# Folding w_phi with 32x32 operands at 16 positions of the TensorE array, in one group per slice

## The chip, the cores and the metric

The program runs on one core of one Trainium2 chip. The metric is device time in microseconds (us): the median of three runs. A profile is one further execution, recorded instruction by instruction; its span is the time from the first to the last instruction.

TensorE multiplies matrices (its rows in the profile are PE, and PEld for loading the stationary operand), VectorE is DVE, ScalarE is ACT, GpSimd is POOL, and SyncE (SP) issues nearly all transfers. The five engines run their own instruction queues in order and wait for each other through semaphores. TensorE writes to PSUM, which has eight banks of 512 f32 columns by 128 partitions.

## The reference

One pre-LayerNorm block: linear attention with a learned feature map, then an MLP with ReLU, both with a residual. B=1, S=2048, D=1024, 32 heads of 32, Dff=3584.

```python
qkv = (x @ wqkv).reshape(B, S, 3, H, Dh)              # x is layernorm(A_x)
pq = einsum("bhsd,hdf->bhsf", q, w_phi)                # w_phi: 32 x 32 per head
pk = einsum("bhsd,hdf->bhsf", k, w_phi)
phi_q = concat([softmax(pq), softmax(-pq)], -1)        # phi_k from pk likewise
kv = einsum("bhsf,bhsd->bhfd", phi_k, v)
z  = einsum("bhsf->bhf", phi_k)
o  = einsum("bhqf,bhfd->bhqd", phi_q, kv) / (einsum("bhqf,bhf->bhq", phi_q, z)[..., None] + 1e-6)
h  = x + o.reshape(B, S, D) @ wo
out = h + relu(layernorm(h) @ w1) @ w2
```

## The kernel before

**Folding.** q and k are used only through w_phi, so the kernel multiplies w_phi into the projection weights: for each head, 1024 x 32 columns of wqkv by a 32 x 32 matrix. This is done on the chip in eight slices p of 256 columns, 0 to 3 for the keys and 4 to 7 for the queries. The weights come transposed (wqkT: one row per output column); a slice is two tiles `wt` of 128 x 1024 (wt_load, L269), a tile holding four heads on its partitions. `bd` (L1125) holds eight block-diagonal 128 x 128 matrices with four heads' w_phi each. fold_mm (L276) makes one block k (128 of the 1024 rows of the weight) of a slice: two f32 matmuls with the 128 x 128 block of wt stationary and bd moving, so the result lies with the weight's rows on the partitions. fold_step (L281) does that into a `tp` bank, and ScalarE copies it to a tile `wp0` (L288, L291 with reordered columns for the queries). fold_store (L296) writes two blocks of 256 KB to a DRAM scratch (wpk or wpq), and fold_ready (L302) marks them as loadable.

**What uses it.** The program is a list of items; an item has eight steps k, and a step is three projection matmuls (mm3, L181 to L183: high x high, high x low, low x high, in a split-f32 format of 512 columns). The first 32 items project the keys and values of the first eight x tiles: slice s by items 8s to 8s+7 (kv_item), then 16 items for the queries, and again for the other eight x tiles. So step 8n+k stands for item n, step k. Weight blocks ("keys" in the class Units) are loaded to six `raw` buffers, split by ScalarE (high part, L124) and by VectorE or GpSimd (low part, L128) into a ring of ten places; a place is freed by the last use in the slice before. At most two places are free ahead of a change of slice, and the other six blocks are split as the old slice's last item lets go of its places.

**What stands beside.** Each kv item ends with kv_first (L409: ScalarE copies the values, VectorE takes maximum, minimum and differences from the bank), then kv_exp, kv_second and kv_z 11, 13 and 18 steps after the item's start, and kv_third (L442: small matmuls) for two or three items together. For the first eight x tiles LayerNorm runs one or two items ahead: ln_stats on VectorE, ln_power on GpSimd, ln_norm on ScalarE (L237), ln_turn on TensorE (L244, into `tp` banks), whose result ScalarE and VectorE split to xT (L177, L178). The table X_STEPS gives the steps of x tiles 1 to 6. GpSimd also makes sums of w1 and w2 blocks (t_sum, L350) between a 512 KB load and a 512 KB store through SP, one every ten steps from step 24, sums 7 to 10 steps after the load.

**What sets the order.** All is placed by hand: do(n, k, f) and when(step, f) attach a function to a step, and it is issued behind that step's three matmuls; within a step functions follow in the order of their registration, before the splits. Every engine runs its instructions in the order in which the program issued them. Fold steps of slices 1 to 7 (L928 to L939) stand at k = 6 of each item from 1 on, and at k = 2 too in items 3 to 5 and from 8 on: 56 in all, the last in item 30. Slice 0 is folded ahead of the first item (first_fold, L371).

PSUM: `mm` has four banks (projection results in turn), `tp` two, `ac` two.

Of the kernel before, what the change touches and what calls it, by code (L numbers as in the profile page):

```python
# [9 lines left out]
F32 = mybir.dt.float32  # L10
F32R = mybir.dt.float32r
AF = mybir.ActivationFunctionType
# [3 lines left out]
P = 128  # L16
# [7 lines left out]
NK = D // P  # L24
# [21 lines left out]
UP = (1, 5, 6, 2, 7, 3, 4)  # L46
DOWN = (1, 5, 6, 3, 7, 2, 4)
OPENS = (1, 5, 2)
BANK_OF = {6: 1, 7: 1, 4: 1, 3: 5}


# [88 lines left out]
def kernel(  # L140
# [12 lines left out]
    v, act, pool, pe, sp = nc.vector, nc.scalar, nc.gpsimd, nc.tensor, nc.sync  # L153
# [26 lines left out]
    def mm3(ps, a_hi, a_lo, b_hi, b_lo, first, last, more=False):  # L180
        pe.matmul(ps, a_hi, b_hi, start=first, stop=False, skip_group_check=more)  # L181
        pe.matmul(ps, a_hi, b_lo, start=False, stop=False, skip_group_check=more)  # L182
        pe.matmul(ps, a_lo, b_hi, start=False, stop=last, skip_group_check=more)  # L183
# [78 lines left out]
    fp = folds.enter_context(tc.tile_pool(name="fold", bufs=2))  # L262
# [3 lines left out]
    wt_of = {}  # L266
# [6 lines left out]
            eng.dma_start(t, wqkT[j])  # L273
            wt_of[p, i] = t

    def fold_mm(p, k, ps):  # L276
        for i in range(2):
            pe.matmul(ps[:, i * P:(i + 1) * P], wt_of[p, i][:, k * P:(k + 1) * P],  # L278
                      bd[:, (2 * p + i) % 8, :], start=True, stop=True)

    def fold_step(p, k):  # L281
        ps = tp_bank()[:, 0:256]
        fold_mm(p, k, ps)
        if k % 2 == 0:
            wp_of[p, k // 2] = fp.tile([P, 512], F32, name="wp0", bufs=3)
        sb = wp_of[p, k // 2][:, k % 2 * 256:(k % 2 + 1) * 256]
        if p < 4:
            act.activation(sb, ps, AF.Copy)  # L288
        else:

            act.activation(sb.rearrange("p (r c f) -> p c r f", r=2, c=4),  # L291
                           ps.rearrange("p (c r f) -> p c r f", r=2, c=4), AF.Copy)

    wp_of = {}

    def fold_store(p, j):  # L296

        r = (p - 4) % 2
        dst = wpk[p][2 * j:2 * j + 2] if p < 4 else wpq[(p - 4) // 2][2 * j:2 * j + 2, :, r * 256:(r + 1) * 256]
        sp.dma_start(dst.rearrange("k p f -> p k f"), wp_of.pop((p, j)).rearrange("p (k f) -> p k f", k=2))  # L300

    def fold_ready(p, j):  # L302

        for k in (2 * j, 2 * j + 1):
            if p < 4 or p % 2:
                folded.add(("kv", p, k) if p < 4 else ("q", (p - 4) // 2, k))

# [61 lines left out]
    first_ps = {}  # L369

    def first_fold(k):  # L371
        if k % 2 == 0:
            first_ps[k // 2] = (ac_bank, mm_bank)[k // 4]()
        fold_mm(0, k, first_ps[k // 2][:, k % 2 * 256:(k % 2 + 1) * 256])

    def first_keys(k):

# [12 lines left out]
        place[0] = k % 2 == 1  # L390

    def first_copy(j):
        wp_of[0, j] = fp.tile([P, 512], F32, name="wp0", bufs=3)
        act.activation(wp_of[0, j], first_ps.pop(j), AF.Copy)

    def ready(key):
        kind, s, k = key[0], key[-2], key[-1]
# [423 lines left out]

    d = {}
# [7 lines left out]
    def d_add(b, m, name, q):  # L830
        v.tensor_add(d[name, q], dbank[b, BANK_OF.get(m, m)][q], d[name, q])

# [23 lines left out]
    for b, tiles in enumerate(groups):  # L856
        for hf in range(2):

            pairs = b == 0 and hf == 0
            for j in range(0, 4, 2 if pairs else 1):  # L860
# [3 lines left out]
                for half in range(2):  # L864
                    n = item(wo_pair, tiles[j:j + 2], hf, half, keys=[("wo", hf, 4 * half + k // 2) for k in range(8)])
# [36 lines left out]
    for t in range(1, NT):  # L902
        n = t - 1 if t < HT else q_n[1, t - HT] + 1
# [19 lines left out]

    for i, j in enumerate((2, 3, 0, 1)):
        do(1 + i // 2, 2 + 4 * (i % 2), first_copy, j)
        when(8 * (1 + i // 2) + 2 + 4 * (i % 2) + 3, fold_store, 0, j)
        when(40, fold_ready, 0, j)
# [12 lines left out]
    assert not todo  # L940


    for (hf, s, t), n in kv_n.items():
# [72 lines left out]
    for u in range(32):  # L1016
        start = 8 * (a0 + u) if u >= 8 else 8 * (last_kv + 4) + 19 * u // 2
# [10 lines left out]
        if u < EARLY:  # L1028
            start = 8 * (kv_n[1, u // 2, NT - 1] + 4 + 4 * (u % 2))
# [81 lines left out]
    wphi = fp.tile([P, 8, 32], F32, name="wphi", bufs=1)  # L1111
# [10 lines left out]
    warm = tp_bank()  # L1122
    for _ in range(16):
        pe.matmul(warm[:, 0:P], ones, ones, start=True, stop=True)
    bd = fp.tile([P, 8, P], F32, name="bd", bufs=1)  # L1125
    v.memset(bd, 0.0)
    for i in range(4):
        r = slice(32 * i, 32 * (i + 1))
        v.tensor_copy(bd[r, :, r], wphi[r])
    ln_stats(("x", 0))  # L1130
    ln_power(("x", 0))
    ln_norm(("x", 0))
# [4 lines left out]
    for k in range(NK):  # L1137
        first_fold(k)
# [66 lines left out]
```

## Time and profile before

| | us |
|---|---|
| runs, median (lowest to highest of three) | 1911.11 (1909.57 to 1911.47) |
| profiled execution, span of the instructions | 1907.8 |
| TensorE busy in the span | 1894.3 (99%) |
| VectorE busy | 1034.8 (54%) |
| GpSimd busy | 974.2 (51%) |
| ScalarE busy | 758.0 (40%) |
| folds: L278, slices 1 to 7, first to last start | 26.3 to 224.4 |

The profiled execution has no time of its own beside the runs; its span lies 3.3 us under their median. Busy is the union of an engine's instructions. Matmuls are pipelined: a row of TensorE lasts from its start to the modelled end of its results, and the next one starts long before; what a matmul takes from the engine is the distance to the next start. In a timeline a row is start, duration, engine, line, operation, out<-in, shape and count (several instructions merged into one row when x is over 1), with the idle time before it and what ended that in brackets. In a group's row the numbers are busy us and mean ns of one, then the idle time before.

### The profile page before, as it was taken

The numbers are of one execution on the slowest core, as the hardware profiler recorded it, in microseconds if no ns is written. First come the engines' busy times: TensorE is split into PE (matmuls) and PEld (weight loads), VectorE is DVE, ScalarE is ACT, GpSimd is POOL, SyncE is SP. The second block draws the span as 40 slices with busy tenths as digits, with TensorE's granted clock in tenths as the row PEclk, the third lists the DMA queues.
The fourth block names the chain that finished last, engine by engine and source line by source line (L and its number), as shares of the span: only waits on it lengthen the run. The fifth ranks groups of instructions, "written<-read, shape, count | busy, mean of one in ns | idle before, by whom it ended". The sixth has DMA issues, their size and how long they took to land.

```text
span 1907.8 us, 31460 instructions
## 1 busy us (share of the span) xinstructions
PE 1894.3 (99%) x11416; PEld 1561.0 (82%) x11416; DVE 1034.8 (54%) x1657; ACT 758.0 (40%) x1314; POOL 974.2 (51%) x961
## 2 busy tenths in 40 slices
PE   9999999999999999999999999999999999999999
PEld 7888888877878888878888888888888888888887
DVE  6666578767679876545644564344433433343333
ACT  5433326222223222245445564444444444444442
POOL 4777752789955988523333222222244444444443
PEclk9999999999999999999999999999999999999999
DMA  6888786666665667796786897566677677767775
GB/s 225 274 267 269 233 273 196 212 192 210 201 196 195 216 206 242 216 303 219 256 252 229 276 294 220 175 195 191 205 255 222 192 239 234 240 212 221 215 215 177
DMA packets 292699, 432.14 MB, mean 227 GB/s; under 512 B 24384, under 2 KB 150336, under 8 KB 292544
## 3 DMA queue, kind: packets, MB, share of 16 engines
q1 hardware_dynamic: 275648, 413.36, 68.5%
q10 hardware_dynamic: 16896, 16.78, 2.6%
q8 instruction: 89, 1.46, 0.3%
q14 instruction: 66, 0.54, 0.1%
HBM read 292.68 MB, written 137.36 MB: 225 GB/s over the span
## 4 chain that ended last, share of the span: by engine, by line
PE 88%; POOL 5%; DMA 4%; issue 1%; DVE 1%; SPq 1%; ACT 0%; POOLq 0%; DVEq 0%; ACTq 0%
PE mm L181 22%; PE mm L182 22%; PE mm L183 22%; PE ac L181 4%; PE ac L182 4%; PE ac L183 4%; PE tp L182 2%; PE tp L183 2%; PE tp L181 2%; POOL b L350 2%; POOL w L128 2%; PE tp L244 1%; PE tp L278 1%; DMA b<-in_w_dram 1%; DMA t<-b 1%
## 5 line engine op out<-in xcount | busy, mean ns | idle before, releaser
L128 POOL TENSOR_TENSOR w<-raw,w 128x512 fp32r<-128x512 f32 x355 | 474.5, 1338 | 725.6 <-ACT w L124 683.2
L124 ACT ACTIVATE w<-raw 128x512 fp32r<-128x512 f32 x686 | 409.3, 626 | 510.8 <-PE mm L183 247.4
L128 DVE TENSOR_TENSOR w<-raw,w 128x512 fp32r<-128x512 f32 x331 | 270.3, 817 | 531.1 <-ACT w L124 527.9
L181 PE MATMUL mm<-w,xT 128*128 128x512 f32 x768 | 311.9, 406 | 0.0
L182 PE MATMUL mm<-w,xT 128*128 128x512 f32 x768 | 301.0, 392 | 3.3 <-POOL w L128 2.9
L183 PE MATMUL mm<-w,xT 128*128 128x512 f32 x768 | 300.6, 391 | 0.0
L182 PE MATMUL mm<-hT,w 128*128 128x512 f32 x672 | 261.7, 389 | 1.3 <-DVE hT L741 1.3
L181 PE MATMUL mm<-hT,w 128*128 128x512 f32 x672 | 262.7, 391 | 0.0
L183 PE MATMUL mm<-hT,w 128*128 128x512 f32 x672 | 261.7, 389 | 0.0
L350 POOL TENSOR_TENSOR b<-b 128x256 f32<-128x256 f32 x224 | 181.9, 812 | 89.7 <-DMA b<-in_w_dram 74.2
L182 PEld LDWEIGHTS mm<-w,xT 128*128 128x128 f32 x768 | 145.0, 189 | 33.6 <-POOL w L128 5.1
L181 PEld LDWEIGHTS mm<-w,xT 128*128 128x128 f32 x768 | 144.9, 189 | 30.8 <-issue 1.7
L183 PEld LDWEIGHTS mm<-w,xT 128*128 128x128 f32 x768 | 144.5, 188 | 30.9
L183 PE MATMUL mm<-w 128*128 128x512 f32 x392 | 152.6, 389 | 0.0
L182 PE MATMUL mm<-w 128*128 128x512 f32 x392 | 152.6, 389 | 0.0
L181 PE MATMUL mm<-w 128*128 128x512 f32 x392 | 152.5, 389 | 0.0
L182 PEld LDWEIGHTS mm<-hT,w 128*128 128x128 f32 x672 | 126.2, 188 | 27.4 <-DVE hT L741 1.7
L183 PEld LDWEIGHTS mm<-hT,w 128*128 128x128 f32 x672 | 126.1, 188 | 26.4
L181 PEld LDWEIGHTS mm<-hT,w 128*128 128x128 f32 x672 | 126.2, 188 | 25.8
L182 PEld LDWEIGHTS mm<-w 128*128 128x128 f32 x392 | 73.6, 188 | 15.3
L183 PEld LDWEIGHTS mm<-w 128*128 128x128 f32 x392 | 73.6, 188 | 15.2
L181 PEld LDWEIGHTS mm<-w 128*128 128x128 f32 x392 | 73.6, 188 | 15.3
(164 smaller groups left out, 3148.6 us busy)
## 6 DMA issues: line engine op xcount, KB each, us to landing
raw<-t SPq DMA_DIRECT2D x224, 256.0 KB, 4.0
raw<-ad SPq DMA_DIRECT2D x196, 256.0 KB, 3.0
raw<-in_w_dram SPq DMA_DIRECT2D x168, 256.0 KB, 3.1
b<-in_w_dram SPq DMA_DIRECT2D x56, 512.0 KB, 4.2
t<-b SPq DMA_DIRECT2D x56, 512.0 KB, 4.2
ad<-c SPq DMA_DIRECT2D x112, 256.0 KB, 3.7
ad<-s SPq DMA_DIRECT2D x84, 256.0 KB, 4.1
ed<-qe ACTq DMA_DIRECT2D x32, 512.0 KB, 4.9
```

What stands on the lines that cost most here:

```text
L124: nc.scalar.activation(w[:, 0, :], raw[1], AF.Copy)
L128: eng.tensor_tensor(out=w[:, 1, :], in0=raw[1], in1=w[:, 0, :].bitcast(F32), op=ALU.subtract)
L181: pe.matmul(ps, a_hi, b_hi, start=first, stop=False, skip_group_check=more)
L182: pe.matmul(ps, a_hi, b_lo, start=False, stop=False, skip_group_check=more)
L183: pe.matmul(ps, a_lo, b_hi, start=False, stop=last, skip_group_check=more)
L244: pe.transpose(pt[:, k, :], xn[:, (4 * j + k) * P:(4 * j + k + 1) * P], ident)
L278: pe.matmul(ps[:, i * P:(i + 1) * P], wt_of[p, i][:, k * P:(k + 1) * P], bd[:, (2 * p + i) % 8, :], start=True, stop=True)
L350: pool.tensor_tensor(out=tsum[j, *out], in0=tsum[j, *a], in1=tsum[j, *b], op=ALU.subtract)
```

## The change

Slices 1 to 7 are folded in one group each, at the steps of the new table FOLD_STEPS. fold_all takes four banks (two of `tp`, or of `ac` for slice 1, and two of `mm`), and for each of the two wt tiles 16 f32 matmuls: the head r's 32 x 32 block of w_phi is stationary, taken from `wphi` itself at partitions 32r, and the moving operand is 32 partitions of wt with every fourth 32 of its 1024 columns (eight pieces, 256 columns). Row r and column q of the 4 x 4 positions give bank r, partitions 32q: the result is the folded weight transposed in blocks of 32 x 32. fold_turn turns it back: for each bank one transpose of VectorE (128 x 512, in blocks of 32 x 32) from PSUM into a tile `wp` of 128 x 8 x 256. That tile has one buffer, where `wp0` had three of a quarter of its size. A slice is stored by one transfer of 1 MB, six steps after its group, is ready 17 steps after, and the next slice's wt is loaded two steps after the group. Slice 0 keeps the old form; its copies go to the same kind of tile. `bd` shrinks to the two matrices of slice 0.

```diff
+FOLD_STEPS = 31, 64, 104, 144, 176, 206, 232
-    def fold_step(p, k):
-        ps = tp_bank()[:, 0:256]
-        fold_mm(p, k, ps)
-        if k % 2 == 0:
-            wp_of[p, k // 2] = fp.tile([P, 512], F32, name="wp0", bufs=3)
-        sb = wp_of[p, k // 2][:, k % 2 * 256:(k % 2 + 1) * 256]
-        if p < 4:
-            act.activation(sb, ps, AF.Copy)
...
+    def fold_all(p):
+
+        banks = [(ac_bank if p == 1 else tp_bank)() for _ in range(2)] + [mm_bank() for _ in range(2)]
+        for i in range(2):
+            wt = wt_of.pop((p, i)).rearrange("p (c q d) -> p c q d", q=4, d=32)
+            for r in range(4):
+                rows = slice(32 * r, 32 * (r + 1))
+                for q in range(4):
+                    pe.matmul(banks[r][32 * q:32 * (q + 1), 256 * i:256 * (i + 1)],
+                              wphi[rows, (2 * p + i) % 8, :], wt[rows, :, q, :], start=True, stop=True)
+        fold_ps[p] = banks
+
+    def fold_turn(p):
+
+        wp_of[p] = wp = fold_tile()
+        for r, ps in enumerate(fold_ps.pop(p)):
+            dst = wp.rearrange("p c (i r f) -> p r i c f", i=2, r=4)[:, r] if p < 4 else \
+                wp.rearrange("p c (e i r f) -> p e r i c f", e=2, i=2, r=2)[:, r % 2, r // 2]
+            v.transpose(dst, ps.rearrange("p (i c d) -> p i c d", i=2, c=8))
+
+    def fold_tile():
+        return fp.tile([P, 8, 256], F32, name="wp", bufs=1)
+
+    def fold_store(p, j=0, n=NK):
...
+        sp.dma_start(dst[j:j + n].rearrange("k p f -> p k f"), wp_of[p][:, j:j + n, :])
...
-    todo = [(p, k) for p in range(1, 8) for k in range(NK)]
-    for n in range(1, 32):
-        for k in ((6,) if n < 8 and n not in (3, 4, 5) else (2, 6)):
-            if not todo:
-                break
-            p, kk = todo.pop(0)
-            do(n, k, fold_step, p, kk)
-            if kk % 2:
-                when(8 * n + k + 3, fold_store, p, kk // 2)
-                when(8 * n + k + 11, fold_ready, p, kk // 2)
-            if kk == 2 and p < 7:
-                do(n, k, wt_load, p + 1, sp)
+    for p, n in enumerate(FOLD_STEPS, 1):
+        when(n, fold_all, p)
+        when(n, fold_turn, p)
+        when(n + 6, fold_store, p)
+        when(n + 17, fold_ready, p)
+        if p < 7:
+            when(n + 2, wt_load, p + 1, sp)
...
-    bd = fp.tile([P, 8, P], F32, name="bd", bufs=1)
+    bd = fp.tile([P, 2, P], F32, name="bd", bufs=1)
```

TensorE's order around the group of slice 1, after step 31 (item 3, k = 7), where before there are single fold steps after steps 30 and 34. Before (tp, mm: PSUM banks; bd, wt: the fold's operands; w, xT: weight block and x tile; xn: normalized x):

```order
L278 MATMUL tp<-bd,wt 128x128 x2
L181 MATMUL mm<-w,xT 128x512
L182 MATMUL mm<-w,xT 128x512
L183 MATMUL mm<-w,xT 128x512
L181 MATMUL mm<-w,xT 128x512
```

Now (the lines of the projection are L182 to L184, and L245 is the turn of an x tile):

```order
L182 MATMUL mm<-w,xT 128x512
L183 MATMUL mm<-w,xT 128x512
L184 MATMUL mm<-w,xT 128x512
L290 MATMUL ac<-wt,wphi 32x256 x8
L290 MATMUL mm<-wt,wphi 32x256 x8
L290 MATMUL ac<-wt,wphi 32x256 x8
L290 MATMUL mm<-wt,wphi 32x256 x8
L182 MATMUL mm<-w,xT 128x512
```

Two matmuls every four or eight steps have become 32 in one piece; eight in a row go to two banks.

VectorE's order at the same place, from kv_second of item 2 (ksm, kphi) to kv_first of item 3 (kmx, ke), the statistics of x tile 6 (st, mv) and the low halves of x tile 5 (xT). Before:

```order
L432 TENSOR_TENSOR kphi<-ke,ksm 128x512
L416 TENSOR_REDUCE kmx<-mm 128x8
L417 TENSOR_REDUCE kmx<-mm 128x8
L419 TENSOR_TENSOR ke<-mm,kmx 128x8x32
L420 TENSOR_TENSOR ke<-kmx,mm 128x8x32
L220 BN_STATS st<-xin 128x6 x2
L222 BN_AGGR mv<-st 128x2
L178 TENSOR_TENSOR xT<-tp,xT 128x512 x2
```

Now:

```order
L444 TENSOR_TENSOR kphi<-ke,ksm 128x512
L300 STREAM_TRANSPOSE wp<-ac 128x2x8x32 x2
L300 STREAM_TRANSPOSE wp<-mm 128x2x8x32 x2
L428 TENSOR_REDUCE kmx<-mm 128x8
L429 TENSOR_REDUCE kmx<-mm 128x8
L431 TENSOR_TENSOR ke<-mm,kmx 128x8x32
L432 TENSOR_TENSOR ke<-kmx,mm 128x8x32
L221 BN_STATS st<-xin 128x6 x2
L223 BN_AGGR mv<-st 128x2
L179 TENSOR_TENSOR xT<-tp,xT 128x512 x2
```

The four transposes stand ahead of kv_first of item 3 and of all that follows it.

SP's order of transfers from the first load of wt behind it (xin: x tiles; b and t: blocks and sums of w1 and w2; wpk: the scratch of the folded keys; raw: weight buffers). Before:

```order
L273 DMA wt<-in_wqkT_dram 128x1024 x2
L214 DMA xin<-in_x_dram 128x1024
L300 DMA wpk_75<-wp_769 128x2x256
L313 DMA raw<-wpk_75 128x256
L314 DMA raw<-in_wv_dram 128x256
```

Now:

```order
L274 DMA wt<-in_wqkT_dram 128x1024 x2
L351 DMA b<-in_w_dram 128x4x256
L311 DMA wpk_75<-wp 128x8x256
L364 DMA t_0_310<-b 512x1x256
L351 DMA b<-in_w_dram 128x4x256
L364 DMA t_0_310<-b 512x1x256
L324 DMA raw<-wpk_75 128x256
L325 DMA raw<-in_wv_dram 128x256
```

The slice leaves by one store of all eight blocks, and the loads that read it come later in the queue.

More of the change, by code (lines that the diff above doesn't have):

```diff
@@ L274, in wt_load, with fold_mm @@
             wt_of[p, i] = t
-    def fold_mm(p, k, ps):
+    def fold_mm(k, ps):
         for i in range(2):
-            pe.matmul(ps[:, i * P:(i + 1) * P], wt_of[p, i][:, k * P:(k + 1) * P],
-                      bd[:, (2 * p + i) % 8, :], start=True, stop=True)
-    def fold_step(p, k):
-        ps = tp_bank()[:, 0:256]
-        fold_mm(p, k, ps)
-        if k % 2 == 0:
-            wp_of[p, k // 2] = fp.tile([P, 512], F32, name="wp0", bufs=3)
-        sb = wp_of[p, k // 2][:, k % 2 * 256:(k % 2 + 1) * 256]
-        if p < 4:
-            act.activation(sb, ps, AF.Copy)
-        else:
-            act.activation(sb.rearrange("p (r c f) -> p c r f", r=2, c=4),
-                           ps.rearrange("p (c r f) -> p c r f", r=2, c=4), AF.Copy)
@@ L294 @@
-    wp_of = {}
-    def fold_store(p, j):
+            pe.matmul(ps[:, i * P:(i + 1) * P], wt_of[0, i][:, k * P:(k + 1) * P],
+                      bd[:, i, :], start=True, stop=True)
+    def fold_all(p):
[8 more added lines that the diff above has]
+        fold_ps[p] = banks
@@ L298, in fold_store, with fold_ready @@
         r = (p - 4) % 2
[L299 to L304, printed above, removed]
+        dst = wpk[p] if p < 4 else wpq[(p - 4) // 2][:, :, r * 256:(r + 1) * 256]
+        sp.dma_start(dst[j:j + n].rearrange("k p f -> p k f"), wp_of[p][:, j:j + n, :])
+    def fold_ready(p):
+        for k in range(NK):
@@ L392, in first_copy @@
     def first_copy(j):
-        wp_of[0, j] = fp.tile([P, 512], F32, name="wp0", bufs=3)
-        act.activation(wp_of[0, j], first_ps.pop(j), AF.Copy)
+        if 0 not in wp_of:
+            wp_of[0] = fold_tile()
+        act.activation(wp_of[0][:, 2 * j:2 * j + 2, :].rearrange("p k f -> p (k f)"), first_ps.pop(j), AF.Copy)
     def ready(key):
@@ L925 @@
         do(1 + i // 2, 2 + 4 * (i % 2), first_copy, j)
[L926 to L940 removed]
+        when(8 * (1 + i // 2) + 2 + 4 * (i % 2) + 3, fold_store, 0, 2 * j, 2)
+    when(40, fold_ready, 0)
+    for p, n in enumerate(FOLD_STEPS, 1):
[5 more added lines that the diff above has]
+            when(n + 2, wt_load, p + 1, sp)
     for (hf, s, t), n in kv_n.items():
```

5 lines of the change are left out of this document (3 added, 2 removed).

## The prediction

> **What bounds the kernel now.** First the page's busy times and the windows, then the groups, the timelines and the chain of waits.
>
> ```profile
> PE 1894.3 (99%) x11416; PEld 1561.0 (82%) x11416; DVE 1034.8 (54%) x1657; ACT 758.0 (40%) x1314; POOL 974.2 (51%) x961
> core 0: us, PE busy (x) PEld busy (x) DVE busy (x) ACT busy (x) POOL busy (x), PEclk, DMA share, GB/s
> 25.00:50.00 25.00, 24.85 (x178) 20.68 (x177) 19.39 (x41) 15.07 (x27) 10.90 (x19) 1.00 0.69 217
> 125.00:150.00 25.00, 25.00 (x154) 21.01 (x154) 18.48 (x39) 7.46 (x17) 17.76 (x24) 1.00 0.88 299
> ```
>
> TensorE is busy 99% of the span, and in these two windows of the folds' stage (9 to 225 us) all but without a break and at the full clock, while VectorE stands at 74 and 78% (18.48 and 19.39 of 25) and the DMA engines at 0.69 and 0.88. So a microsecond taken from TensorE here is a microsecond of the end, unless something else arrives too late for the earlier TensorE. The price of one fold step of today shows in a timeline of TensorE:
>
> ```profile
> 79.06 0.39 PE L181 MATMUL mm<-w,xT 128*128 128x512 f32 x1
> 79.29 0.39 PE L182 MATMUL mm<-w,xT 128*128 128x512 f32 x1
> 79.52 0.39 PE L183 MATMUL mm<-w,xT 128*128 128x512 f32 x1
> 79.75 0.60 PE L278 MATMUL tp<-bd,wt 128*128 128x128 f32 x4
> 80.11 0.48 PE L181 MATMUL mm<-w,xT 128*128 128x512 f32 x1
> 80.42 0.40 PE L182 MATMUL mm<-w,xT 128*128 128x512 f32 x1
> L278 PE MATMUL tp<-bd,wt 128*128 128x128 f32 x224 | 33.9, 274 | 0.0
> ```
>
> Matmuls overlap, so I read starts, not durations. Projection matmuls start every 0.23 us. From L183 at 79.52 to L182 at 80.42 are 0.90 us, where two plain distances would be 0.453: the step costs **0.447 us**. An f32 matmul leaves two records, so 224 records are 112 matmuls, 56 steps.
>
> **The change part by part.** *Removed from TensorE*: 56 x 0.447 = **25.0 us**.
>
> *Added to TensorE*: seven groups of 32 matmuls, each 32x32 with 256 moving columns. Attention (L620) already works on 16 positions in f32, with 128 columns and 64 matmuls in one piece:
>
> ```profile
> 573.60 0.39 PE L183 MATMUL mm<-w,xT 128*128 128x512 f32 x1
> 573.92 0.34 PE L620 MATMUL tp<-qe,kvL 32*32 32x128 f32 x8
> 574.67 0.26 PE L620 MATMUL tp<-qe,kvL 32*32 32x128 f32 x1
> 575.10 0.26 PE L620 MATMUL tp<-qe,kvL 32*32 32x128 f32 x1
> 575.75 0.50 PE L181 MATMUL mm<-w,xT 128*128 128x512 f32 x1
> 576.09 0.39 PE L182 MATMUL mm<-w,xT 128*128 128x512 f32 x1
> ```
>
> From 573.60 to 576.09 are 2.49 us, less 0.453: the piece costs 2.04 us. A round over the 16 positions takes 0.43 us (574.67 to 575.10), four rounds 1.72, and 0.32 is entry and exit. The entry is 0.32 from L183 to the first L620, where the fold step above has 0.23. A fold group has two rounds of twice the columns, which no row shows. Lower bound: a round is set by the issue of its 32 records and stays at 0.43, so 2 x 0.43 + 0.32 = 1.18. Upper bound: a round doubles, 2 x 0.86 + 0.32, and the last stream ends 0.11 later (128 columns take that long: four L278 records span 0.60 and one lasts 0.27, so their starts are 0.33 / 3 apart), 2.15. I take **1.65**, the middle: records of one position must follow each other, and they get twice as long, but the other positions run beside them. Seven groups: **11.6 us** (8.3 to 15.0). TensorE gains 25.0 - 11.6 = 13.4 (10.0 to 16.7).
>
> [...]
>
> *Moved from ScalarE to VectorE.* 56 evacuations go (L291, L288), and 28 transposes of 128x512 from PSUM come:
>
> ```profile
> L291 ACT ACTIVATE wp<-tp 128x256 f32<-128x256 f32 x32 | 12.3, 384 | 59.7 <-PE tp L278 55.3 <-issue 4.1
> L606 DVE STREAM_TRANSPOSE qe<-qe 128x1024 f32<-128x1024 f32 x28 | 34.4, 1233 | 16.4 <-POOL qe L600 14.7 <-POOL qe L590 1.8
> L178 DVE TENSOR_TENSOR xT<-tp,xT 128x512 fp32r<-128x512 f32 x32 | 21.4, 677 | 12.9 <-ACT xT L177 12.8
> ```
>
> ScalarE loses 56 x 0.38 = 21 us of work; it is not the bound, worth 0. A transpose of 512 columns costs between half of 1.23 (0.62) and a whole (1.23); I take 0.69, the nearest row that reads 512 f32 columns from PSUM, so 2.8 us a group and 19 in all (17 to 34). They stand at the head of VectorE's queue until the group is through, so VectorE also waits. Behind them come kv_first of the last item, the statistics of a coming x tile and the low halves of xT. Between the folds this is hidden: the bank that a delayed kv_first frees is wanted an item later at the earliest (24 x 0.23 = 5.5 us), and in the order behind the other six turns stand softmax steps and statistics, no split of L128. Uncovered, each group would cost up to 2.8 plus the wait.
>
> At the first group it is not hidden, and the stage is bound there by another chain:
>
> ```profile
> 31.28 0.60 PE L244 MATMUL tp<-ident,xn 128*128 128x128 f32 x4
> 31.92 0.60 ACT L177 ACTIVATE xT<-tp 128x512 fp32r<-128x512 f32 x1 [0.23 <-PE tp L244]
> 36.47 1.24 ACT L237 ACTIVATE xn<-xin,sc 128x1024 f32<-128x1024 f32 x1 [1.65 <-POOL sc L231]
> 37.22 0.40 PE L183 MATMUL mm<-w,xT 128*128 128x512 f32 x1
> 37.77 0.66 PE L244 MATMUL tp<-ident,xn 128*128 128x128 f32 x4
> 42.88 0.41 DVE L416 TENSOR_REDUCE kmx<-mm 128x8 f32<-128x256 f32 x1
> 44.21 1.27 DVE L220 BATCH_NORM_STATS2 st<-xin 128x6 f32<-128x512 f32 x2
> 47.69 1.24 ACT L237 ACTIVATE xn<-xin,sc 128x1024 f32<-128x1024 f32 x1 [0.20 <-POOL sc L231]
> 51.61 0.60 PE L244 MATMUL tp<-ident,xn 128*128 128x128 f32 x4
> ```
>
> TensorE already waits at 37.77 (0.55 after L183, not 0.23) for the normalized x tile 4, whose chain starts with the turn at 31.28 and can move forward by 0.23 at most, ScalarE's own wait. Three fold steps before it go (1.34 us), so 1.1 is lost. Then the group: TensorE would come to the turn of x tile 6 at 51.61 - 0.23 - 3 x 0.447 (steps 30, 34, 38) + 1.65 = 51.7. VectorE reaches the transposes near 42.8 and is through 2.8 later, so the statistics of 44.21 move to 47.0, ScalarE's norm from 47.69 to 50.5, and the tile is there at 51.8. That is 0.1 or 0.2 late. Start: **1.3 us** lost (0 to 2.5).
>
> *Later weights.* TensorE reaches the change of weight slices sooner. The tightest one between folds is key 6 of slice 2:
>
> ```profile
> 119.34 1.29 POOL L128 TENSOR_TENSOR w<-raw,w 128x512 fp32r<-128x512 f32 x1 [3.96 <-ACT w L124]
> 127.67 1.29 POOL L128 TENSOR_TENSOR w<-raw,w 128x512 fp32r<-128x512 f32 x1
> 129.86 0.39 PE L182 MATMUL mm<-w,xT 128*128 128x512 f32 x1
> ```
>
> GpSimd ends it at 128.96, 0.90 before TensorE reads it. The chain of GpSimd (119.34 to 128.96) keeps its length, three fold steps of TensorE beside it go (1.34): **0.4 us** lost (0 to 2.5).
>
> *Stores and loads.* Four stores of 256 KB become one of 1 MB on SP's queue, issued 6 steps after the group, which waits for the turn. Behind it in that queue stand the loads and stores of the sums of w1 and w2, the x tiles and the weight loads:
>
> ```profile
> b<-in_w_dram SPq DMA_DIRECT2D x24, 512.0 KB, 4.5
> wpk<-wp SPq DMA_DIRECT2D x16, 256.0 KB, 4.2
> xin<-in_x_dram SPq DMA_DIRECT2D x17, 512.0 KB, 5.7
> ```
>
> At 299 GB/s (the window above) 1 MB takes 3.5 us, so I expect it to land in 6 to 8. Loads of the fold's keys may follow 11 steps (7.5 us) after the store, and are first used 16 steps after that: hidden. Uncovered it is the wait of GpSimd for a load of b, part of the 2.5 above. wt loads stand two steps after each group, 30 before use: hidden. The smaller bd ends 1 us earlier at a place where VectorE waits for x anyway: 0.
>
> **Sum**: 13.4 - 1.3 - 0.4 = 11.7 us. The profiled span is 1907.8, so 1896.1; the median of the runs is 1911.1, 3.3 above the span, so **1899.4**.
>
> **The rivals.** (A) *The group is cheap and nothing is late*: 25.0 - 8.3 - 0.5 = 16.2, 1894.9. For it: L620's first round is through in 0.32. Against: the wait at 37.77. (B) *The group is at its upper price*, 2.15, with 3.5 lost at start and slices: 25.0 - 15.0 - 3.5 = 6.5, 1904.6. For it: 256 columns double each stream. (C) *Slower: the turn holds VectorE.* If the transposes cost 1.23 and stand waiting for the group, all behind them is late by 4 x 1.23 + 1.65 = 6.6 us, seven times. It decides from (25.0 - 11.6) / 7 = 1.9 us of TensorE's waits a group; at 3 us it is 7 x 4.65 - 25.0 = +7.6, 1918.7. For it: VectorE at 74 to 78% in two windows. Against: banks and splits have 4 us and more of room after the start. [...] (D) *The gain is waited away*: GpSimd's splits and late loads of b take all but 2 us, 1909. For it: DMA at 0.88 and 1 MB bursts. Against: 0.90 us of room even at the tightest split. (E) *The positions don't run side by side* with 256 columns: 64 records of 0.22 (twice 0.11) are 14 a group, 98 - 25 = +73, 1984. Against: L620's 128 records start within 1.7 us.
>
> **How the numbers follow.** Chances: forecast 0.52, A 0.15, B 0.16, C 0.07, D 0.07, E 0.03. Faster by over 0.2% (3.8 us, what can be told from no change) are the first three, 0.83; the same, D, 0.07; slower, C and E, 0.10. The range from A to a little past B, 1894 to 1906.5, holds 0.8.
>
> **What would show it.** In the new profile: from the last L183 before a group to the second projection matmul behind it 1.65 + 0.45 us; transposes near 0.69; a wait of TensorE for xn near 37.5 of over 1 us; a wait for GpSimd's split at the first item of slice 2 of about 0.4; no other wait before 230 us, and the same distance from there to the end. A group over 2.2 us, transposes over 1 us, or waits of TensorE behind every turn would prove me wrong.

## The result: the time stays where it was

| | median, us | range of the runs, us | profiled execution, us |
|---|---|---|---|
| before | 1911.81 | 1909.26 to 1916.80 (12 runs) | 1907.8 |
| changed | 1912.12 | 1910.00 to 1916.25 (12 runs) | 1910.0 |

The ratio of changed to before is 1.0002, with a 95% interval of 0.9993 to 1.0011: no difference that can be told. Forecast were 1899.4 us and a range of 1894 to 1906.5; the result lies outside it and is that of rival D, "the gain is waited away", which had a chance of 0.07.

**What came as forecast.** The page of the changed kernel gives its span:

```profile
span 1910.0 us, 31857 instructions
```

The second fold group stands in the timeline of TensorE as follows (start, duration, line; x8 is eight records in one row, and an f32 matmul leaves two: the group's 32 are 64 records here):

```profile
69.75 0.39 PE L184 MATMUL mm<-w,xT 128*128 128x512 f32 x1
70.06 0.45 PE L290 MATMUL tp<-wt,wphi 32*32 32x256 f32 x8
...
71.07 0.49 PE L290 MATMUL mm<-wt,wphi 32*32 32x256 f32 x8
71.49 0.50 PE L182 MATMUL mm<-w,xT 128*128 128x512 f32 x1
71.83 0.40 PE L183 MATMUL mm<-w,xT 128*128 128x512 f32 x1
```

From the last projection matmul before the group to the second one behind it are 2.08 us, 0.45 of them the two matmul distances that are there anyway: a group costs 1.63 us, where 1.65 was forecast. The turns on VectorE, by the tile's own view (count, then shortest, median and longest in ns):

```profile
L300 DVE STREAM_TRANSPOSE wp<-mm x14: 668/674/675, 43.7 to 217.0; 128x512 f32<-128x512 f32 x14
L300 DVE STREAM_TRANSPOSE wp<-tp x12: 668/689/717, 74.3 to 215.8; 128x512 f32<-128x512 f32 x12
```

That is the 0.69 of the forecast. So the operations cost what they were taken to cost.

**Where the gain went.** The start of a step can be counted off in a trace: step n begins with projection matmul number n of the first of mm3's three lines. Counted so, in us (the last three columns are experiments, below):

| step | before | changed | e1 | e3 | e6 |
|---|---|---|---|---|---|
| 48 | 57.55 | 56.40 | 56.61 | 56.34 | 56.47 |
| 128 | 125.06 | 119.95 | 119.29 | 119.00 | 119.13 |
| 144 | 138.59 | 144.45 | 138.10 | 137.15 | 131.50 |
| 256 | 231.67 | 232.11 | 225.78 | 227.06 | 219.22 |
| 336 | 289.48 | 292.45 | 286.98 | 286.69 | 277.98 |

Up to step 128 the changed kernel is 5.1 us ahead. In the next 16 steps it loses 11.0. Behind them it gains again, 5.4 us up to step 256. One place eats the gain, then, the change to slice 2 at step 128. A smaller loss follows where the queries begin: from step 256 to step 336 the changed kernel loses 2.5 us more. TensorE's waits in the first 330 us (total us, times, longest), for a low half of a weight block in the kernel before, and then for the same and for a normalized x tile in the changed kernel:

```profile
PE mm L182 <- POOL w L128: 1.0, 2, 0.8
```

```profile
PE mm L183 <- POOL w L129: 12.3, 7, 8.4
PE tp L245 <- ACT xn L238: 2.8, 2, 1.7
```

In the timeline of the changed kernel, TensorE first and then GpSimd (in brackets the idle time before an instruction and what ended it):

```profile
122.91 0.50 PE L183 MATMUL mm<-w,xT 128*128 128x512 f32 x1 [1.21 <-POOL w L129]
...
124.18 0.39 PE L182 MATMUL mm<-w,xT 128*128 128x512 f32 x1
132.93 0.80 PE L183 MATMUL mm<-w,xT 128*128 128x512 f32 x1 [8.37 <-POOL w L129]
...
133.96 0.63 PE L182 MATMUL mm<-w,xT 128*128 128x512 f32 x1
134.38 0.63 PE L183 MATMUL mm<-w,xT 128*128 128x512 f32 x1
...
138.66 0.39 PE L184 MATMUL mm<-w,xT 128*128 128x512 f32 x1
```

```profile
121.60 1.26 POOL L129 TENSOR_TENSOR w<-raw,w 128x512 fp32r<-128x512 f32 x1
127.75 1.12 POOL L361 TENSOR_TENSOR b<-b 128x256 f32<-128x256 f32 x1 [4.89 <-DVE mv L223]
...
131.17 1.71 POOL L129 TENSOR_TENSOR w<-raw,w 128x512 fp32r<-128x512 f32 x1
...
134.34 1.28 POOL L129 TENSOR_TENSOR w<-raw,w 128x512 fp32r<-128x512 f32 x1
```

TensorE waits 8.4 us for the low half of a weight block that GpSimd makes from 131.17 on. GpSimd had not been busy before: it stands from 122.9 to 127.75 at a sum of w1 (L361), and the split is behind that sum in its queue. The bracket names VectorE, whose statistics of an x tile end at 127.72 too; but the sum reads only b, and its block b, loaded from 122.22 on, landed 5.4 us later, at 127.6. The other two sums in the stretch that waited for their load began 0.1 us after its landing as well. SyncE's timeline shows why that load was late. L351 loads a b, L364 stores one (rows of other transfers are left out):

```profile
93.56 0.43 SPq L351 DMA_DIRECT2D b<-in_w_dram  x1
94.09 0.52 SPq L364 DMA_DIRECT2D t<-b  x1
100.90 0.38 SPq L351 DMA_DIRECT2D b<-in_w_dram  x1
...
106.54 0.53 SPq L364 DMA_DIRECT2D t<-b  x1
...
112.91 0.38 SPq L351 DMA_DIRECT2D b<-in_w_dram  x1
...
114.41 0.53 SPq L364 DMA_DIRECT2D t<-b  x1
...
122.22 0.38 SPq L351 DMA_DIRECT2D b<-in_w_dram  x1
```

There are two buffers for b, so the load at 100.90 had to wait until the store at 94.09 had landed (6.8 us after its issue), that at 112.91 for the store at 106.54 (6.4), and that at 122.22 for the store at 114.41 (7.8). The last of these loads belongs to step 114, which began at 108.5: it is 13.7 us late. SyncE's waits between 54 and 140 us, before and then changed, show the same:

```profile
SPq L340 <- DMA t<-b: 4.3, 5, 2.0
```

```profile
SPq L351 <- DMA t<-b: 35.5, 6, 8.2
```

A buffer's round in the changed kernel: loaded at 93.56, summed from 99.5 to 103.9, stored at 106.54, loaded again at 112.91: 19.3 us for two sums. The program asks for a sum every ten steps, and the 20 steps from 84 to 104 last 14.6 us in it. In the kernel before the same round was 16.1 us, and those steps lasted 16.9:

```profile
87.52 0.38 SPq L340 DMA_DIRECT2D b<-in_w_dram  x1
...
99.42 0.52 SPq L353 DMA_DIRECT2D t<-b  x1
...
103.61 0.38 SPq L340 DMA_DIRECT2D b<-in_w_dram  x1
```

At this round the loop of b just kept up with the old pace, and it would be too slow for the new one. The round is no fixed size, though: counted from one load of a buffer to its next, the first 16 rounds last from 12.0 to 24.1 us before and from 12.6 to 23.6 in the changed kernel. Part of the longer rounds is the landing of the stores; here from issue to landing, between 54 and 140 us, before and then changed (times, KB each, median us):

```profile
t<-b SPq DMA_DIRECT2D x10, 512.0 KB, 4.4
```

```profile
t<-b SPq DMA_DIRECT2D x9, 512.0 KB, 6.4
```

What shows the loop falling behind is the issue of its loads against the steps that they belong to (us late; SyncE can also run ahead of TensorE):

| load | 4th | 5th | 6th | 7th | 8th | 9th | 10th | 11th |
|---|---|---|---|---|---|---|---|---|
| before | -1.3 | -3.6 | 1.1 | -0.5 | -1.3 | -1.3 | 1.0 | 6.9 |
| changed | 3.1 | 4.9 | 6.5 | 8.2 | 8.7 | 12.9 | 13.7 | 19.4 |

### The profile page after: what moved, and what is told of

It is laid out like the page before. It is cut to its first block, busy times and chain, and to the rows that moved or that the text cites. A ratio compares the mean times of both kernels' runs of the same rounds, so it can differ in the third digit from the quotient of the medians.

```text
span 1910.0 us, 31857 instructions
## 1 busy us (share of the span) xinstructions
PE 1884.6 (99%) x11640; PEld 1540.9 (81%) x11640; DVE 1045.3 (55%) x1685; ACT 739.2 (39%) x1258; POOL 975.8 (51%) x961
## 4 chain that ended last, share of the span: by engine, by line
PE 83%; POOL 7%; DMA 6%; issue 1%; DVE 1%; SPq 0%; ACT 0%; POOLq 0%; DVEq 0%; ACTq 0%
PE mm L182 21%; PE mm L183 21%; PE mm L184 21%; PE ac L183 4%; PE ac L184 4%; PE ac L182 4%; POOL b L361 3%; DMA b<-in_w_dram 3%; PE tp L183 2%; PE tp L184 2%; PE tp L182 2%; POOL w L129 2%; DMA t<-b 2%; DMA xin<-in_x_dram 1%; PE tp L245 1%
## 5 line engine op out<-in xcount | busy, mean ns | idle before, releaser
L182 PE MATMUL mm<-w,xT 128*128 128x512 f32 x768 | 309.3, 403 | 0.0
L184 PE MATMUL mm<-w,xT 128*128 128x512 f32 x768 | 301.2, 392 | 0.0
L182 PE MATMUL mm<-hT,w 128*128 128x512 f32 x672 | 262.7, 391 | 0.0
L184 PE MATMUL mm<-hT,w 128*128 128x512 f32 x672 | 261.6, 389 | 0.0
L361 POOL TENSOR_TENSOR b<-b 128x256 f32<-128x256 f32 x224 | 181.5, 810 | 99.2 <-DMA b<-in_w_dram 84.5
L183 PEld LDWEIGHTS mm<-w,xT 128*128 128x128 f32 x768 | 145.3, 189 | 48.9 <-POOL w L129 19.1
L182 PEld LDWEIGHTS mm<-w,xT 128*128 128x128 f32 x768 | 145.2, 189 | 35.1 <-issue 4.2
L184 PEld LDWEIGHTS mm<-w,xT 128*128 128x128 f32 x768 | 145.2, 189 | 30.7
L182 PE MATMUL mm<-w 128*128 128x512 f32 x392 | 152.5, 389 | 0.0
L184 PE MATMUL mm<-w 128*128 128x512 f32 x392 | 152.5, 389 | 0.0
L184 PEld LDWEIGHTS mm<-hT,w 128*128 128x128 f32 x672 | 126.1, 188 | 26.4
L182 PEld LDWEIGHTS mm<-hT,w 128*128 128x128 f32 x672 | 126.1, 188 | 26.0 <-ACT c L776 0.3
L436 ACT ACTIVATE ke<-ke 128x512 f32<-128x512 f32 x64 | 40.4, 631 | 121.2 <-DVE ke L432 121.2
L182 PEld LDWEIGHTS mm<-w 128*128 128x128 f32 x392 | 73.6, 188 | 15.3
L183 PEld LDWEIGHTS mm<-w 128*128 128x128 f32 x392 | 73.6, 188 | 15.3
```

The costliest lines, as they stand in the source:

```text
L361: pool.tensor_tensor(out=tsum[j, *out], in0=tsum[j, *a], in1=tsum[j, *b], op=ALU.subtract)
L436: act.activation(e_of[key], e_of[key], AF.Exp)
```

## The experiments

Three theories stood at the start. **Theory 1**, the loop of b: two buffers and the landing of the stores set its pace, the faster steps outrun it, SyncE and GpSimd stand at its waits, and the weight splits behind them come late. **Theory 2**, bursts: stores of 1 MB beside 1 MB of wt make all transfers near them slower. **Theory 3**: VectorE's turns, which a bracket seemed to name, delay the chain. The "8.8 us" of the expectations is the distance of two starts (124.18 to 132.93) in which the 8.4 us of waiting lie. By "the changed kernel" 1912 us is meant; where a difference is small the ratio to the kernel before, from the same series, decides.

### A third buffer for b (e1_third_b)

```diff
-            t = fp.tile([P, D], F32, name="wt", bufs=4)
+            t = fp.tile([P, D], F32, name="wt", bufs=2)
...
-        b = tsp.tile([P, 4, 256], F32, name="b", bufs=2)
+        n = 2 * (NP * (w - 1) + p) + j
+        if n < 18 and n % 3 == 2:
+            b = fp.tile([P, 4, 256], F32, name="b3", bufs=1)
+        else:
+            b = tsp.tile([P, 4, 256], F32, name="b", bufs=2)
...
+    when(10, wt_load, 1, sp)
...
-    wt_load(1, sp)
```

> The changed kernel with a third buffer for b (the sums of w1 and w2) while the fold lasts; the room comes from two wt buffers instead of four, with the second pair of wt loaded at step 10 instead of before the first projection. Theory 1 (the loop of b is the limit: load of b about 5.5 us, four sums 4.3, store 6.5, so a buffer is busy 16 us and two buffers give a sum every 8 us, while ten steps of TensorE now last 7): with three buffers a sum can come every 5.4 us, GpSimd does not wait for b, the wait of 8.8 us at 124 us and the half clock behind it go, and the time is 1912 - 11 = 1901 (1897 to 1904). Theory 2 (the stores of 1 MB lengthen every transfer near them): the stores are still there, the load of b still lands late, 1909 to 1912. Theory 3 (VectorE's turns are what delays the weights): 1912.

Measured: 1904.87 us, ratio 0.9962 (0.9949 to 0.9975). SyncE's wait for a store of b is gone from the stretch of 54 to 140 us, and what is left there is:

```profile
SPq L324 <- POOL w L129: 18.8, 4, 9.7
SPq L368 <- POOL b L365: 14.9, 4, 5.9
```

TensorE's wait at the change of slice is 4.8 us instead of 8.4. Theories 2 and 3 had no change; theory 1 had 1901 (1897 to 1904) and got two thirds of it, just outside its range. GpSimd still stood for a load of b, which was issued behind the 1 MB store of a slice (L311) and took 8.7 us to land:

```profile
109.69 0.80 SPq L311 DMA_DIRECT2D wpk<-wp  x1
...
113.17 0.55 SPq L355 DMA_DIRECT2D b<-in_w_dram  x1
```

```profile
117.00 1.73 POOL L129 TENSOR_TENSOR w<-raw,w 128x512 fp32r<-128x512 f32 x1
122.05 1.16 POOL L365 TENSOR_TENSOR b<-b 128x256 f32<-128x256 f32 x1 [3.33 <-DMA b<-in_w_dram]
```

So the load's place in SyncE's queue and the burst before it were both still open.

### The store in four pieces (e2_stores_split)

```diff
-        when(n + 6, fold_store, p)
+        for j in range(4):
+            when(n + 6 + 2 * j, fold_store, p, 2 * j, 2)
```

> The changed kernel with the store of a folded group in four pieces of 256 KB, two steps apart, instead of one of 1 MB. Theory 1 (loop of b): the loop is as before, the wait at 124 us stays within 2 us of its 8.8, 1912 (1909 to 1914). Theory 2 (bursts): the stores of b land in 4.5 us again instead of 6.5, the wait goes below 3 us, 1903 (1900 to 1906). Theory 3: 1912.

Measured: 1909.91 us, ratio 0.9994 (0.9984 to 1.0004), which can't be told from the changed kernel. Stores of b landed in 5.6 us instead of 6.4 (medians between 54 and 140 us; 4.4 in the kernel before), but TensorE's wait stayed:

```profile
PE mm L183 <- POOL w L129: 13.9, 8, 6.7
```

Theory 2 had 1903 and a wait below 3 us. As the main cause it falls.

### The loop of b 12 steps later (e3_b_later)

```diff
-        step = 24 + 10 * n
+        step = 24 + 10 * n + (12 if n >= 3 else 0)
```

> The changed kernel with the loads, sums and stores of b from the fourth on 12 steps later in the order; nothing else is moved. Theory 1: the loads, which are up to 19 us late against their steps, are then 8 us less late, so GpSimd and SP stand less where they wait for b; the wait at 124 us falls below 3 us and the time is 1904 (1900 to 1908). Theory 2: the same bursts meet the same splits, 1911 to 1913.

Measured: 1904.77 us, ratio 0.9966 (0.9953 to 0.9978), as theory 1 had it; the longest wait for a split is 2.1 us. The fold's groups, turns and stores keep their steps: it is enough that the sums are asked for nearer to the time at which they can come. The loop has not caught up, though. Its tenth load is still 13.2 us behind its own, later step, where 8 us less were expected; but its sum no longer stands ahead of the split that TensorE waits for there, and SyncE's waits for stores of b fall from 35.5 to 11.3 us.

### The old pace with all the new parts (e4_old_pace)

```diff
+    old = [8 * n + k for n in range(1, 32) for k in ((6,) if n < 8 and n not in (3, 4, 5) else (2, 6))][:56]
+    for step in old[::2]:
+        when(step, pace)
```

where pace() issues two f32 matmuls of 128x128 on the identity into a tp bank.

> The changed kernel with two f32 matmuls of 128x128 into a bank of PSUM that nobody reads, at every second of the 56 old fold steps: TensorE gets 28 x 0.447 = 12.5 us of work back and runs at about the pace of the kernel before, with the new groups, turns and 1 MB stores kept. Theory 1: at the old pace the loop of b keeps up, the wait of 8.8 us at 124 us goes below 2 us, and the time stays where it is: 1912 (1909 to 1914). Theory 2 and theory 3: bursts and turns are still there, the wait stays, and the added work comes on top: 1920 to 1925.

Measured: 1916.72 us, ratio 1.0025 (1.0016 to 1.0034), between the two forecasts. Its waits of TensorE in 330 us:

```profile
PE mm L183 <- POOL w L129: 3.9, 3, 3.0
PE tp L298 <- DVE wp L306: 2.8, 2, 1.4
```

The long wait went from 8.4 to 3.0 us (theory 1 had below 2) with bursts and turns in place, and 12.5 us of added work cost 4.6; that is theory 1's side. The 2.8 us in the second row are the experiment's own: the added matmuls wait for a bank that VectorE still turns. The rest is not accounted for, so the time alone would not have decided.

### A third buffer in the kernel before (e5_before_third_b)

```diff
-        b = tsp.tile([P, 4, 256], F32, name="b", bufs=2)
+        n = 2 * (NP * (w - 1) + p) + j
+        if n < 18 and n % 3 == 2:
+            b = fp.tile([P, 4, 256], F32, name="b3", bufs=1)
+        else:
+            b = tsp.tile([P, 4, 256], F32, name="b", bufs=2)
```

and two wp0 tiles instead of three, wphi in one of them.

> The kernel before with the third buffer for b of e1_third_b; for the room, two wp0 tiles instead of three and wphi in one of them. Theory 1 (two buffers give a sum every 8 us, which is just the pace of ten steps in the kernel before, 7.7 to 8): the loop holds back the change, not the kernel before, which waits only 2.9 us for GpSimd's splits in all; it gains 0 to 3 us, 1908 to 1911. Rival (a third buffer is worth the same in any kernel): 6 us, 1905.

Measured: 1918.06 us, ratio 1.0042 (1.0029 to 1.0055), slower, which neither forecast had. It loses at the start, where the longest wait of TensorE is for a bank that ScalarE has not yet copied out to one of the two wp0 tiles (ScalarE itself waits 5.2 us there for a store out of such a tile):

```profile
45.33 1.11 PE L244 MATMUL tp<-ident,xn 128*128 128x128 f32 x4 [4.22 <-ACT wp L288]
```

Step 32 begins 9.0 us later than in the kernel before. From there to step 336 it takes 247.3 us against 247.6. In the stretch in which the third buffer is worth 6 us to the changed kernel, it is worth 0.3 to the kernel before; as a whole the run proves little, and e12 asks a like question with an edit that takes no room.

### The loads six steps earlier (e6_third_b_early), and group 3 too (e7_and_group_3_early)

e6, on top of e1:

```diff
-        when(step, t_load, w, p, j)
+        when(step - 6 if n < 18 else step, t_load, w, p, j)
```

> The kernel of e1_third_b with the loads of b six steps (4.1 us) earlier as long as there are three buffers; in e1_third_b the wait at 122 us is still 4.8 us, and the load of b before it is issued 4.4 us late and lands 8.9 us after. If the place of the load in SP's order is what is left (theory 1): the wait at 122 us falls below 1.5 us and the time is 1901 (1899 to 1903). If the 1 MB store, issued 3.5 us before that load, is what is left (theory 2, smaller than first thought): the load still lands late, the wait stays above 3 us, 1904 (1903 to 1906).

e7, on top of e6:

```diff
-FOLD_STEPS = 31, 64, 104, 144, 176, 206, 232
+FOLD_STEPS = 31, 64, 92, 144, 176, 206, 232
```

> The kernel of e6_third_b_early with the third fold group at step 92 instead of 104, so that its 1 MB store and the next 1 MB of wt are issued 12 steps (8 us) further from the change to slice 2. Theory 1: nothing left to gain there, within 1.5 us of e6_third_b_early. Theory 2: what is left of the wait at 122 us goes, 1900 (1898 to 1902), 2 to 4 us below e6_third_b_early.

Measured: e6 1896.32 us, ratio 0.9927 (0.9915 to 0.9939); e7 1896.23 us, ratio 0.9923 (0.9911 to 0.9936). Both are faster than either kernel of this study, and 13 us below the kernel before. Theory 1 had the wait of e6 (below 1.5 us; the longest is now 0.7) and that e7 adds nothing, but its time for e6 was 1901 (1899 to 1903), some 3 us too little gain even at its lower end. TensorE's waits in 330 us of e6, and below them SyncE's between 54 and 140 us:

```profile
PE tp L245 <- ACT xn L238: 2.4, 2, 1.3
PE mm L183 <- POOL w L129: 1.5, 4, 0.7
```

```profile
SPq L355 <- DMA t<-b: 1.1, 1, 1.1
```

So the rest in e1 is mended by the place of the load in SyncE's order. Whether it stood late because of that place or because of the burst, these two runs don't tell: in e6 the load is issued at 104.95, ahead of the 1 MB store at 105.39, where in e1 it came behind it (113.17 after 109.69). With the load already in front, moving the store away in e7 makes no difference. The table above shows the gap closing: steps 128 to 144 take 12.4 us in e6, 24.5 in the changed kernel, 13.5 before.

### Group 3 early, nothing else (e8_group_3_early)

The edit of e7 on the changed kernel itself.

> The changed kernel with nothing else than the third fold group at step 92 instead of 104. Theory 1: b has two buffers, so the loop falls behind as before, the wait at 124 us stays above 6 us, 1912 (1909 to 1914). Theory 2 (bursts next to the change of slice): the wait falls below 3 us, 1905 (1902 to 1907).

Measured: 1909.82 us, ratio 1.0003 (0.9993 to 1.0013), no change, as theory 1 had it. Its profile agrees only in part, with

```profile
PE mm L183 <- POOL w L129: 8.1, 6, 3.1
```

The longest wait is shorter than theory 1 said: steps 128 to 144 take 18.6 us instead of 24.5, and the tenth load is 8.1 us late instead of 13.7. So the place of the group, with its turns, its store and the next wt, does add to the loss there. The loss comes back elsewhere: steps 256 to 272 take 18.9 us against 14.3 in the changed kernel. The loop is still behind (its eleventh load by 13.1 us); why it costs so much more at step 256 was not followed up.

### The loss without the change (e9_before_every_nine)

The kernel before, with the loop asked to run nearly as fast, in us, as the changed kernel asks it:

```diff
-        step = 24 + 10 * n
+        step = 24 + 9 * n if n < 24 else 10 * n
```

> The kernel before with the loop of b every 9 steps instead of every 10 for its first 24 turns; no part of the change is in it. Theory 1 (two buffers give a sum every 8 us): 9 steps of the kernel before last 7.05 us, as 10 steps of the changed one, so the loop falls behind here too, its loads are over 8 us late by the tenth, TensorE waits over 4 us for GpSimd's splits between 110 and 145 us, and the time is 1916 (1913 to 1921). Rival (the loss needs the groups, the turns or the 1 MB stores): 1911 (1908 to 1912).

Measured: 1927.38 us, ratio 1.0081 (1.0061 to 1.0101). No group, turn or store of 1 MB is in this kernel, and it loses 16.5 us; the tenth load is 11.2 us late, although its stores of b land in 4.6 us, about as in the kernel before. (Nine steps last 7.6 us between steps 84 and 104, not the 7.05 of the expectation; ten of the changed kernel last 7.3.) TensorE's waits in 330 us, then SyncE's between 54 and 140 us:

```profile
PE mm L182 <- POOL w L128: 12.2, 7, 3.8
```

```profile
SPq L340 <- DMA t<-b: 21.2, 8, 5.3
```

Steps 128 to 144 take 19.1 us instead of 13.5. The place is that of the changed kernel, and the order is the same: GpSimd's sum waits for its load until 127.66, and the split behind it (130.72 to 132.43) is what TensorE waits for until 132.47. Later places come on top (steps 192 to 208 take 20.4 instead of 13.5), which theory 1's number (1913 to 1921) had left out. By step 256 12.6 us are lost; behind its 24th turn this edit also asks for the loads 24 steps earlier than before, so the rest of the loss says less.

### Stores of b by GpSimd (e10_pool_stores_b)

```diff
-        sp.dma_start(td[w, p][:, :, 256 * j:256 * (j + 1)], tsum[j])
+        pool.dma_start(td[w, p][:, :, 256 * j:256 * (j + 1)], tsum[j])
...
-        when(step + 13, t_store, w, p, j)
+        when(step + 10, t_store, w, p, j)
```

> The changed kernel with the stores of b issued by GpSimd right behind the fourth sum, instead of by SP three steps later in SP's order; two buffers as in the changed kernel. In the changed kernel SP issued the stores of the seventh and eighth b 2.6 and 4.9 us after their sums had ended, since it stood at another wait. Theory 1 with the stress on how long a buffer is held: 3 us less of 16, a sum every 6.5 us, the wait at 124 us falls below 3 us, 1904 (1901 to 1907), plus what GpSimd pays to issue. Theory 1 with the stress on the loads' place in SP's order: the loads still stand behind SP's other waits, 1910 (1907 to 1914).

Measured: 1929.87 us, ratio 1.0095 (1.0080 to 1.0111); both forecasts missed. GpSimd pays for the issue itself (busy us and mean ns, then the idle time before):

```profile
L364 POOL DMA_DIRECT2D t<-b x56 | 41.7, 744 | 18.0 <-POOL b L361 17.7 <-DMA b<-in_w_dram 0.3
```

These are about 1.1 us for each b, on the engine whose splits are already late. But most of the 18 us is not lost beside the fold: at step 336 this kernel is only 2.8 us behind the changed one, and between 400 and 500 us TensorE is idle for 8.5 us against 1.5. So the run says little on theory 1, and what it loses there was not followed up.

### Earlier loads with two buffers (e11_two_b_early)

The edit of e6 on the changed kernel, without the third buffer.

> The changed kernel with two buffers for b and the loads six steps earlier for the first 18, as in e6_third_b_early but without its third buffer. Theory 1: a load cannot start before the store two turns back has landed, so SP only stands longer at it and holds up the loads of weights behind: 1913 (1910 to 1920). Rival (only the place of the loads counts, not the buffer): 1898 to 1902.

Measured: 1922.20 us, ratio 1.0058 (1.0040 to 1.0076). SyncE between 54 and 140 us:

```profile
SPq L351 <- DMA t<-b: 52.8, 9, 8.3
```

A load that was put ahead in SyncE's queue, and could not go, held all behind it here: 52.8 us of such waits against 35.5 in the changed kernel. Theory 1 had the sign, and 2 us too little loss even at its upper end. In these runs the earlier place is worth something only with the third buffer.

### The kernel before with the loop later (e12_before_b_later)

The edit of e3 on the kernel before.

> The kernel before with the loads, sums and stores of b from the fourth on 12 steps later, the edit that took 7 us from the changed kernel in e3_b_later. Theory 1: the loop keeps up in the kernel before, whose waits for GpSimd's splits are 2.9 us in all, so 0 to 3 us can be gained, 1909 (1908 to 1911.5). Rival (the place of these sums costs any kernel the same, and the fold has little to do with it): 1904.

Measured: 1907.96 us, ratio 0.9987 (0.9978 to 0.9996): 2 us (theory 1 had 1908 to 1911.5), where the same edit takes 7 from the changed kernel. The loop held back the change, and hardly the kernel before.

## Why the prediction was wrong

**Removed steps and the group's price** (25.0 and 11.6): right. Groups cost 7 x 1.63 = 11.4 us, and the kernel in which TensorE waits only 1.5 us for splits (e6) is 13.2 us under the kernel before by the medians, 11.5 of them by step 336, where the sum had 11.7. That was the right size for a gain of TensorE that is let through. The reason given for the middle of the two bounds, that the records of one position follow each other while other positions run beside them, was the author's estimate; what the trace shows is the 1.63 us of a group.

**The turns at nothing** and **the start at 1.3 us**: right in kind. In e6, with all turns in place, no wait of TensorE in 330 us is for VectorE. At the start TensorE waits 1.11 us for the normalized x tile 4, as worked out:

```profile
37.28 0.66 PE L245 MATMUL tp<-ident,xn 128*128 128x128 f32 x4 [1.11 <-ACT xn L238]
```

At step 48 eight fold steps (3.58) have gone and one group (1.63) has come, so 1.95 should be gained and 1.15 are: 0.8 lost. The second part of the 1.3, a late x tile 6, does not come: TensorE does not wait before its turn at 51.38.

**Later weights at 0.4 us (0 to 2.5)**: this step failed. It took the split at 127.67 us, found 0.90 us of room in it, and let "the chain of GpSimd (119.34 to 128.96)" keep its length; a load of b that comes late was named and priced as "part of the 2.5". The chain did not keep its length: with a load of b in it that came at 127.7 us, its last split ended at 135.6 instead of 128.96, while TensorE's use had moved 5 us forward. In the runs' numbers the term is 8.37 + 1.21 us of waits and about 2.7 us at a granted clock of 0.50, 12.3 in all, and it nearly equals the gain. With the 0.8 of the start and the 2.5 between steps 256 and 336 that is 15.6 of the 16.6 us by which step 336 comes later than 25.0 - 11.4 alone would have it. Room was measured at one instruction, in the trace of the old pace, for a loop whose lateness adds up. The right question was the pace: a sum every 8.0 us in the round shown (16.1 / 2) against ten steps that last 8.4 us before and 7.3 behind the change, in that stretch. As an estimate from these, ten turns at 0.7 us too little are 7 us, many times the room of 0.90; the tenth load came 13.7 us late. The load at step 124 is already 6.9 us late in the kernel before, a warning that no sentence weighed.

**Stores and loads "hidden"**: right for the fold's own stores. No wait of TensorE names them, and SyncE waits 5.2 us for them in 330 us, though the two between 54 and 140 us landed in 9.9 us (median), where 6 to 8 were expected. Bursts were not needed for a loss at this place (e9), and thinning or moving them left the time where it was (e2, e7, e8); but stores of b landed 2.0 us later beside them, and moving a group with its transfers took 5.9 us from the place (e8). They seem to add to the lateness of the loop; how much of the 13.7 us is theirs is open.

**The rivals.** D is what happened, in its outcome and its engine: it names GpSimd's splits and late loads of b, and it was given 0.07. The bursts that were named for it were not needed, and the "0.90 us of room even at the tightest split" that spoke against it was the wrong measure, as was the "4 us and more of room" for banks and splits under C. A's group of 1.18 us is not in the trace. That its time is near that of the kernel with the loop mended (1894.9 against 1896.3) is luck: as a gain, e6's 13.2 lies nearer to the forecast's 11.7 than to A's 16.2. B's group of 2.15, C's waits behind every turn and E's 14 us a group find nothing in the trace.

Not settled are how the loop's lateness, and e1's remaining wait, divide between the buffers, the queue's order and the transfers beside it, and what e10 lost beyond the issuing. In e1, e6 and e7 the second pair of wt is also loaded later and into two buffers instead of four; that part was not run alone.

## What to carry to other kernels

When the bounding engine is made faster, look up every loop that runs beside it at a fixed number of its steps, and compare that loop's own round (load, work, landing of the store, divided by its buffers) with the new length of those steps. Look at how late its loads already are, and whether that grows, and not only at the room before one instruction. Here a loop just at its pace turned a gain into a wait somewhere else, because the splits that TensorE needed stood in one queue with its sums. The remedy was a buffer more and the load put far enough ahead to use it; the second without the first made it worse.

## What the runs showed of the hardware

**The long waits here cost more than their length.** After the 8.4 us in which TensorE stood, most starts of projection matmuls lie 0.43 us apart instead of 0.23 (133.96 and 134.38 above), until 138.4. The windows of the changed kernel (busy us of the five engines with their counts, then granted clock, DMA share, GB/s):

```profile
125.00:130.00 5.00, 0.00 (x0) 0.00 (x0) 3.64 (x7) 0.00 (x0) 2.25 (x2) 0.82 0.87 307
130.00:135.00 5.00, 2.07 (x5) 1.69 (x6) 4.11 (x9) 1.15 (x2) 4.92 (x6) 0.50 0.17 51
135.00:140.00 5.00, 5.00 (x16) 3.64 (x15) 2.54 (x5) 0.39 (x1) 4.62 (x7) 0.65 0.98 305
```

The granted clock was 0.50 across the end of the wait, and it stayed halved for 5.5 us of work: the 12 matmuls from 132.93 to 138.40 take 5.47 us, where 12 distances of 0.23 would be some 2.7 us less. In the changed kernel it fell some 3.7 us after the last matmul had ended at 124.57: by windows of 1 us it was 1.00 until 128 us, 0.61 from there to 129, and 0.50 from 129 to 138. In e1 it fell sooner. Its mean there from 120 to 145 us was 0.86, which is some 7 us at half, and the starts are 0.23 apart again from 131.39 on; as an estimate from these it fell some 2 us after the last matmul had ended at 122.44. The way back took 5.5 us here, 4.1 in e1 after a wait of 4.8 (127.28 to 131.39), and 3.2 in e9 after a wait of 3.8 (132.47 to 135.71).

**Positions with 256 columns.** 32 f32 matmuls of 32x32 (64 records) over 16 positions, with 256 columns each, took 1.63 us with entry and exit (69.75 to 71.83 in the changed kernel, less 0.45). As an estimate from the rounds of L620 in the kernel before, two rounds of 128 columns with the same entry and exit would be 1.18 (2 x 0.43 + 0.32), and two rounds of twice the length 2.15 (2 x 0.86 + 0.32, and 0.11 for the end of the last stream). By that a round got longer with its columns here, but less than twice.

**A store issued by GpSimd** kept GpSimd for 0.74 us in e10 (mean of 56), after 0.3 us of waiting for its own last sum (18.0 us in all).
